# Exponentials in neighbouring pairs, eleven heads instead of eighteen with a column of ones, and a new order of steps

## The chip, the core and the metric

The kernel runs on one core of a Trainium2 chip. The metric is the device time of one execution in microseconds (us); of several runs the median counts. A core has five engines that run side by side: TensorE (PE, with its weight loads as a row of their own, PEld), VectorE (DVE), ScalarE (ACT), GpSimd (POOL) and SyncE (SP), which issues the transfers here. Each works through a fixed row of instructions and waits where data or a buffer is missing.

## The reference

The kernel computes pooled attention and then a token and channel mixer:

```python
# q, k, v: (4, 8, 1152, 64); w_tok1 (576, 256), w_tok2 (256, 576), w_ch1 (512, 1536), w_ch2 (1536, 512)
q_pool = q.reshape(B, H, S // 2, 2, D).mean(axis=3)
scores = np.matmul(q_pool, k.transpose(0, 1, 3, 2)) / np.sqrt(D)
attn = np.exp(scores - scores.max(-1, keepdims=True))
attn = attn / (attn.sum(-1, keepdims=True) + 1e-9)
x = (attn @ v).transpose(0, 2, 1, 3).reshape(B, S // 2, H * D)
h = np.maximum(x.transpose(0, 2, 1) @ w_tok1, 0) @ w_tok2
u = x + h.transpose(0, 2, 1)
out = u + np.maximum(u @ w_ch1, 0) @ w_ch2          # (4, 576, 512)
```

There are 32 heads (4 batches of 8) with 1152 keys, 576 pooled queries and 64 channels each.

## The kernel before, in words

All matrix products run in a 32-bit format that keeps fewer bits of each number than float32, so each operand is split into a high part and the rest, and a product is the sum of two or three matmuls.

**A head.** The keys stand in 9 chunks of 128, the queries in two halves of 288. One step `s` of `main` (0 to 8) takes two of the 18 pairs of half and chunk. PE computes the scores of each pair with keys on the partitions (line 756, two matmuls of 288 columns; the second also subtracts the row's maximum). ACT takes the exponential twice: once as full float32 into the tile PF (called `pf`, line 766), once rounded into `ph` (line 769). DVE or POOL forms the rest `pl = pf - ph` (line 773; the helper `both` leaves the choice of the engine to the plan). PE then multiplies `ph` and `pl` with the values `vv` (line 798) and adds up over the 9 chunks in the PSUM tile `o`.

**The sum over keys**, which divides each row, is had in two ways. Heads in the list `IN_PV` put a column of ones into `vv`: POOL saves the column that was there in `V0` and overwrites it (lines 615 and 617), and PE needs a third matmul of 288 columns for each pair, with that saved column as its one-column weight (`o<-ph,v`, 18 in a head). The others let DVE add up the 9 chunks in PF, in three thirds of 96 queries for each half (`tensor_reduce`, line 780, 6 in a head); since this leaves one number for each of the 128 partitions, PE adds these up with a column of ones (line 827, 5 matmuls in a head, each of which stands as two instructions in the trace). IN_PV has 18 heads: 0 to 3 and the odd ones from 5 to 31.

`finish` turns the result back (line 820, 5 matmuls, two instructions each), and DVE computes the denominator `den`, its reciprocal `rd` and the scaled result `u` (lines 832 to 842). The maxima of the rows are found ahead of each head by matmuls (line 691) into a ring of three PSUM tiles `r`, which DVE reduces (line 693). After each four heads comes a token mix (lines 858 to 901): ACT and DVE or POOL split `u` into `big` tiles, PE multiplies with the token weights (line 873), and again (line 891), and DVE adds to `u`. The channel mixer (lines 966 to 1030) comes after all heads.

**The order.** Nothing is issued in the order of the code. `step` records each operation with an engine, an assumed cost, a due time and the data it reads and writes. `Plan.run` then places the steps, earliest start first and due time next, and so writes each engine's row when the program is built. The table `DUE` at the head of the file shifts the due times. POOL steps and those DVE steps that are marked `shared` are planned so that they don't overlap. On the chip each engine follows its row and waits for semaphores.

Of the kernel before, what the change touches and what calls it, by code (L numbers as in the profile page):

```python
# [10 lines left out]
F32 = mybir.dt.float32  # L11
# [3 lines left out]
ALU = mybir.AluOpType  # L15
AX = mybir.AxisListType
# [6 lines left out]
PE, ACT, DVE, POOL, DMA, HOST = range(6)  # L23
# [7 lines left out]


DUE = {
    "scores": -1.4,
    "p_lo": 0.02,
    "sum": -2.82,
    "pv": 1.78,
    "o": -107.46,
    "finish": 5.54,
    "max": -22.72,  # L40
    "max_each": 0.53,
    "prep": -32.49,
    "v": 9.58,
    "stack": 29.51,
    "stack_2": 96.51,
    "mix": 9.83,
    "mix_x": 6.03,
    "w_tok": -27.04,
    "w_tok_each": 7.34,
    "sum_each": 1.2,  # L50
    "pv_lo": 0.54,
    "lo_first": 7.78,
    "max_first": -120.52,
    "max_second": 37.69,
    "scores_each": -10.71,
    "p_hi": 0.84,
    "pv_one": -0.04,
    "finish_each": -14.96,
    "den_sum": -47.39,
    "x_lo": 5.05,  # L60
    "x": -54.79,
    "den": -45.22,
    "rd": -27.39,
    "u": 18.75,
    "u_each": 75.19,
    "max_of": 7.22,
    "max_row": -32.02,
    "max_first_each": -127.47,
    "q_pool": -3.78,
    "q_turn": 1.79,  # L70
    "k_each": 1.45,
    "k_hi": -42.28,
    "k_lo": 1.7,
    "q_hi": -79.72,
    "q_lo": 70.53,
    "load_kq": -48.02,
    "load_v": -163.1,
    "v_lo": -10.5,
    "load_w_tok": 117.45,
    "mix_x_lo": 3.96,  # L80
    "mix_1": 3.17,
    "mix_t": 2.11,
    "mix_2": 2.45,
    "mix_u": -79.91,
    "w_ch": 235.24,
    "w_ch_each": -64.39,
    "ut_0": -4.75,
    "ut_1": -50.96,
    "stay": 0.78,
}  # L90


# [145 lines left out]
def kernel(  # L238
# [24 lines left out]
    P = 128  # L263
    SQ = S // 2
    NK = S // P
# [16 lines left out]
    due = DUE  # L282
    WARM = 8
    KEEP = (0, 1, 2, 3)
    UNSTACKED = 1
    IN_PV = (0, 1, 2, 3, *range(5, 32, 2))
    CUT = 3
    FOLDS = 114
    LO = (None,) * 9
# [25 lines left out]
        return 65 + 0.521 * n  # L315

    def pool_(n):
        return 150 + 2.1 * n

    def both(n, fn, *args, on=None):  # L320

# [89 lines left out]
    QD = many(early, 2, [P, P], F32R, "qd")  # L411
    MH = fix.tile([P, P], F32R, name="mh")
    OT = many(fix, 2, [P, SQ], F32, "ot")
    PF = fix.tile([P, 2 * NK, HF], F32, name="pf")
    SUM = fix.tile([P, 2, HF], F32, name="sum")
    REST = words(SUM).rearrange("p f x -> p (f x)")[:, 0:2 * J]

# [316 lines left out]
    def main(h, t0):  # L734
        i3, i2 = h % 3, h % 2
        stacked = [(KK[i3], QQ[i3]), (K2[i2][0:D + 1], Q2[i2][0:D + 1])]
        ready = [(x, i3, y) for x in ("qq", "kk") for y in range(2)] + [("k2", i2), ("q2", i2)]

        plain = [(x[0:D], y[0:D]) for x, y in (
            (KHI, QHI[0]), (KLO, QHI[0]), (KHI, QLO[0]))]  # L740
        plain.append((K2[0][D:D + 1], Q2[0][D:D + 1]))
        seen = [(x, y) for x in ("kh", "kl") for y in range(3)]
        seen += [(x, 0, y) for x in ("qh", "ql") for y in range(2)]
        for s in range(NS):
            t = t0 + s
            units = [divmod(2 * s + i, NK) for i in range(2)]
            st = Buf("s")
            for i, (fq, c) in enumerate(units):
                terms, read = stacked, ready
                if h == 0 and s < UNSTACKED:  # L750
                    terms, read = plain, seen
                read = read + [("row", i2, x) for x in ((0, 1, 2), (2, 3, 4))[fq]]

                def scores(st=st, i=i, fq=fq, c=c, terms=terms):
                    for n, (w, x) in enumerate(terms):
                        te.matmul(  # L756
                            at(st)[:, i, 0:HF], w[:, c * P:(c + 1) * P],
                            x[:, fq * HF:(fq + 1) * HF],
                            start=(n == 0), stop=(n == len(terms) - 1))

                step(PE, len(terms) * mm(HF), scores, t + due["scores"] + i * due["scores_each"],
                     read,
                     [(st, i)], [st] if i == 0 else [])
            ph, pl = Buf("ph"), Buf("pl")
            pf = PF[:, 2 * s:2 * s + 2]
            step(ACT, act_ps(2 * HF), lambda pf=pf, st=st: sc.activation(  # L766
                pf, at(st)[:, :, 0:HF], AF.Exp, scale=ESC), t,
                [(st, 0), (st, 1)], [("pf", s)])
            step(ACT, act_ps(2 * HF), lambda ph=ph, st=st: sc.activation(  # L769
                at(ph), at(st)[:, :, 0:HF], AF.Exp, scale=ESC), t + due["p_hi"],  # L770
                [(st, 0), (st, 1)], [ph], [ph])
            pv = h in IN_PV
            both(2 * HF, lambda e, pf=pf, ph=ph, pl=pl: e.tensor_sub(  # L773
                at(pl), pf, f(at(ph))), t + due["p_lo"], [("pf", s), ph], [pl], [pl],
                on=LO[s])
            if s in (4, NS - 1) and not pv:
                fq = s // 5
                for y in range(CUT):
                    cs = slice(y * HF // CUT, (y + 1) * HF // CUT)
                    step(DVE, 65 + 1.83 * NK * HF // CUT, lambda fq=fq, cs=cs: ve.tensor_reduce(  # L780
                        SUM[:, fq, cs],
                        PF[:, fq * NK:(fq + 1) * NK, cs].rearrange("p c x -> p x c"),
                        axis=AX.X, op=ALU.add), t + due["sum"] + y * due["sum_each"],
                        [("pf", x) for x in range(fq * 4, fq * 4 + 5)], [("sum", fq, y)])
            for i, (fq, c) in enumerate(units):
                if c == 0:
                    o, parts = Buf("o"), []
                terms = [(ph, VV[i2], P), (pl, VV[i2], P)]
                if pv:
                    terms.insert(1, (ph, V0[i2], 1))  # L790
                for n, (x, w, m) in enumerate(terms):
                    new, end = not parts, (c, n) == (NK - 1, len(terms) - 1)
                    key = (o, "new") if new else (o, c, n)
                    read = [x, ("v0" if m == 1 else "vv", i2)]
                    if not new:
                        read += parts if end else parts[:1]
                    step(PE, mm(HF),
                         lambda o=o, x=x, w=w, m=m, i=i, c=c, new=new, end=end: te.matmul(  # L798
                             at(o)[0:m], w[:, c], at(x)[:, i], start=new, stop=end),
                         t + due["pv"] + (x is pl) * due["pv_lo"] + (m == 1) * due["pv_one"], read, [key], [o] if new else [])  # L800
                    parts.append(key)
                if c == NK - 1:
                    step(ACT, act_ps(HF), lambda o=o, fq=fq: sc.copy(  # L803
                        OT[i2][:, fq * HF:(fq + 1) * HF], at(o)), t + due["o"],
                        parts, [("ot", i2, fq)])
# [321 lines left out]
```

## Time and profile before

| | |
|---|---|
| Three runs | 962.26, 963.37, 965.88 us (median 963.37) |
| The profiled execution | 965.31 us |
| Its span, first to last instruction | 963.5 us |
| Mean granted clock of TensorE | 0.978 of full speed |
| Busy | PE 97%, DVE 73%, ACT 53%, POOL 37% |
| 0 to 60 us | start: first head, weights of the token mix |
| 60 to 640 us | heads 1 to 31 and the token mixes |
| 640 to 963.5 us | last token mix, channel mixer |

The busy time of PE counts matmuls from start to end, and they overlap in the pipeline. So PE reads as busy even where small gaps lie between the starts. What a matmul costs is read from the distance of the starts in the timeline, not from its duration.

### The profile page before, as it was taken

The numbers are of one execution on the slowest core, as the hardware profiler recorded it, in microseconds if no ns is written. First come the engines' busy times: TensorE is split into PE (matmuls) and PEld (weight loads), VectorE is DVE, ScalarE is ACT, GpSimd is POOL, SyncE is SP. The second block draws the span as 40 slices with busy tenths as digits, with TensorE's granted clock in tenths as the row PEclk, the third lists the DMA queues.
The fourth block names the chain that finished last, engine by engine and source line by source line (L and its number), as shares of the span: only waits on it lengthen the run. The fifth ranks groups of instructions, "written<-read, shape, count | busy, mean of one in ns | idle before, by whom it ended". The sixth has DMA issues, their size and how long they took to land.

```text
span 963.5 us, 15874 instructions
## 1 busy us (share of the span) xinstructions
PE 934.6 (97%) x5852; PEld 845.2 (88%) x5852; DVE 703.5 (73%) x1268; ACT 514.3 (53%) x1038; POOL 353.4 (37%) x309
## 2 busy tenths in 40 slices
PE   9979899999999999999999999999999999999997
PEld 4767799899999999888899999998999999999996
DVE  6799999899899899989998989988882212121211
ACT  1657687687677676776766767755441111111110
POOL 0444366584584673655655646330000000000000
PEclk7789999999999999999999999999999999999999
DMA  6775656465465475365454533124430101000001
GB/s 137 202 171 121 138 113 146 97 141 126 95 151 118 93 162 118 87 136 117 100 127 95 125 69 87 45 89 133 151 110 1 66 1 33 0 34 0 32 2 33
DMA packets 89844, 91.54 MB, mean 95 GB/s; under 512 B 43884, under 2 KB 68840, under 8 KB 89768
## 3 DMA queue, kind: packets, MB, share of 16 engines
q1 hardware_dynamic: 89768, 90.54, 38.9%
q8 instruction: 46, 0.75, 0.3%
q14 instruction: 30, 0.25, 0.1%
HBM read 43.25 MB, written 4.72 MB: 50 GB/s over the span
## 4 chain that ended last, share of the span: by engine, by line
PE 77%; DVE 17%; ACT 3%; DMA 2%; issue 1%; DVEq 0%; SPq 0%; ACTq 0%
PE r L988 16%; PE o L798 14%; PE s L1016 12%; PE s L756 10%; PE r L691 7%; DVE mx L693 6%; DVE pl L773 3%; PE r L820 3%; PE r L891 3%; DVE sum L780 3%; PE o L1016 3%; PE r L873 2%; PE r L827 2%; DMA kk<-kl 1%; PE r L559 1%
## 5 line engine op out<-in xcount | busy, mean ns | idle before, releaser
L773 POOL TENSOR_TENSOR pl<-pf,ph 128x576 fp32r<-128x576 f32 x187 | 267.7, 1452 | 155.2 <-ACT ph L769 107.7
L766 ACT ACTIVATE pf<-s 128x576 f32<-128x576 f32 x288 | 189.4, 659 | 87.6 <-PE s L756 80.3
L693 DVE TENSOR_REDUCE mx<-r 128x1 f32<-128x384 f32 x384 | 198.6, 553 | 17.3 <-PE r L691 14.5
L769 ACT ACTIVATE ph<-s 128x576 fp32r<-128x576 f32 x288 | 187.9, 659 | 0.0
L756 PE MATMUL s<-qq,kk 128*128 128x288 f32 x574 | 169.8, 308 | 1.8 <-ACT ph L769 1.6
L756 PE MATMUL s<-q,k 65*128 65x288 f32 (+1 forms) x576 | 167.4, 302 | 0.0
L996 DVE SCALAR_TENSOR_TENSOR h<-r,h 128x384 fp32r<-128x384 f32 x72 | 40.1, 557 | 166.9 <-ACT h L994 166.8
L780 DVE TENSOR_REDUCE sum<-pf 128x96 f32<-128x864 f32 x84 | 147.4, 1763 | 0.9 <-ACT pf L766 0.8
L798 PE MATMUL o<-ph,vv 128*128 128x288 f32 x576 | 145.5, 307 | 0.9 <-ACT ot L803 0.9
L691 PE MATMUL r<-kk,qq 128*128 128x384 f32 x372 | 131.7, 369 | 14.1 <-DVE mx L693 6.8
L994 ACT ACTIVATE h<-r 128x384 fp32r<-128x384 f32 x72 | 35.4, 492 | 197.0 <-PE r L988 196.8
L798 PE MATMUL o<-pl,vv 128*128 128x288 f32 x576 | 139.4, 299 | 0.3 <-DVE pl L773 0.3
L1016 PE MATMUL s<-w,h 128*128 128x512 f32 x504 | 130.8, 394 | 0.0
L756 PEld LDWEIGHTS s<-qq,kk 128*128 128x128 f32 x574 | 110.8, 193 | 6.0 <-ACT ph L769 4.0
L756 PEld LDWEIGHTS s<-q,k 65*128 65x128 f32 (+1 forms) x576 | 111.5, 194 | 0.6 <-issue 0.6
L798 PEld LDWEIGHTS o<-ph,vv 128*128 128x128 f32 x576 | 101.2, 192 | 11.1 <-ACT ot L803 2.6
L988 PE MATMUL r<-big,w 128*128 128x384 f32 x576 | 109.0, 337 | 0.0
L1016 PEld LDWEIGHTS s<-w,h 128*128 128x128 f32 x504 | 93.4, 188 | 16.5
L988 PEld LDWEIGHTS r<-big,w 128*128 128x128 f32 x576 | 101.7, 188 | 3.8 <-DVE h L996 0.2
L798 PEld LDWEIGHTS o<-pl,vv 128*128 128x128 f32 x576 | 100.0, 191 | 1.6 <-DVE pl L773 0.6
L773 DVE TENSOR_TENSOR pl<-pf,ph 128x576 fp32r<-128x576 f32 x101 | 93.4, 930 | 2.1 <-ACT ph L769 1.5
L691 PEld LDWEIGHTS r<-kk,qq 128*128 128x128 f32 x372 | 71.4, 195 | 26.3 <-DVE mx L693 10.7
(129 smaller groups left out, 1274.7 us busy)
## 6 DMA issues: line engine op xcount, KB each, us to landing
raw<-in_moe_w_ch_dram SPq DMA_DIRECT2D x24, 512.0 KB, 3.8
kk<-kh SPq DMA_DIRECT2D x32, 288.0 KB, 3.4
kk<-kl SPq DMA_DIRECT2D x32, 288.0 KB, 4.9
qq<-qh SPq DMA_DIRECT2D x64, 144.0 KB
vn<-in_v_dram SPq DMA_DIRECT2D x32, 288.0 KB, 2.8
k<-kk SPq DMA_DIRECT2D x31, 288.0 KB, 5.1
kn<-in_k_dram SPq DMA_DIRECT2D x30, 288.0 KB
qn<-in_q_dram SPq DMA_DIRECT2D x32, 256.0 KB, 7.6
```

The source lines that it names most:

```text
L691: step(PE, mm(SP3), lambda ps=ps, w=w, x=x: te.matmul(at(ps)[:, 0:SP3], w, x, start=True, stop=True), t, read, [ps], [ps])
L693: step(DVE, dve(SP3), lambda ps=ps, m=m: ve.tensor_reduce(m, at(ps)[:, 0:SP3], axis=AX.X, op=ALU.max), t + due["max_of"], [ps], [key])
L756: te.matmul(at(st)[:, i, 0:HF], w[:, c * P:(c + 1) * P], x[:, fq * HF:(fq + 1) * HF], start=(n == 0), stop=(n == len(terms) - 1))
L766: step(ACT, act_ps(2 * HF), lambda pf=pf, st=st: sc.activation(pf, at(st)[:, :, 0:HF], AF.Exp, scale=ESC), t, [(st, 0), (st, 1)], [("pf", s)])
L769: step(ACT, act_ps(2 * HF), lambda ph=ph, st=st: sc.activation(at(ph), at(st)[:, :, 0:HF], AF.Exp, scale=ESC), t + due["p_hi"], [(st, 0), ...
L773: both(2 * HF, lambda e, pf=pf, ph=ph, pl=pl: e.tensor_sub(at(pl), pf, f(at(ph))), t + due["p_lo"], [("pf", s), ph], [pl], [pl], on=LO[s])
L780: step(DVE, 65 + 1.83 * NK * HF // CUT, lambda fq=fq, cs=cs: ve.tensor_reduce(SUM[:, fq, cs], PF[:, fq * NK:(fq + 1) * NK, cs].rearrange(" ...
L798: lambda o=o, x=x, w=w, m=m, i=i, c=c, new=new, end=end: te.matmul(at(o)[0:m], w[:, c], at(x)[:, i], start=new, stop=end),
L988: te.matmul(at(ps)[:, 0:GT], w[:, c], x[:, c], start=(c == 0 and n == 0), stop=(c == NC4 - 1 and n == 2))
L994: step(ACT, act_ps(GT), lambda: sc.activation(at(h)[:, 0], at(ps)[:, 0:GT], AF.Relu), t, [ps], [h])
L996: step(DVE, dve(GT), lambda: ve.scalar_tensor_tensor(out=at(h)[:, 1], in0=at(ps)[:, 0:GT], scalar=0.0, in1=f(at(h))[:, 0], op0=ALU.max, op ...
L1016: te.matmul(at(ps), a[:, x * P:(x + 1) * P], w, start=(fi == 0 and m == 0), stop=(fi == NF - 1 and m == 2))
```

## The change

It has four parts.

1. PF gets a last dimension of two: the exponentials of the same query of two neighbouring chunks lie side by side. ACT writes each of its two chunks with a distance of 8 bytes from element to element, and `pl` reads PF with the same distance. The middle step (`s == 4`), whose two chunks belong to different halves, gets two places of its own, each with a second element that is set to zero once at the start (a new memset of 576 elements).
2. DVE's sum runs over the five pairs of a half, so over 10 elements for each query in place of 9, with the two of a pair next to each other.
3. IN_PV keeps heads 0 to 3 and every fourth from 5 to 29: 11 heads, not 18. Seven heads go from the column of ones to the sum on DVE, among them head 31, the last.
4. The table of due times has other numbers, and the planner's assumed cost of POOL's elementwise operations is 2.3 ns an element, not 2.1.

```diff
 DUE = {
-    "sum": -2.82,
+    "sum": -2.85,
...
-    "p_hi": 0.84,
+    "p_hi": -1.72,
...
-    IN_PV = (0, 1, 2, 3, *range(5, 32, 2))
+    IN_PV = (0, 1, 2, 3, *range(5, 32, 4))
...
     def pool_(n):
-        return 150 + 2.1 * n
+        return 150 + 2.3 * n
...
-    PF = fix.tile([P, 2 * NK, HF], F32, name="pf")
+
+
+    PF = fix.tile([P, 2 * 5, HF, 2], F32, name="pf")
+    ve.memset(PF[:, 4:6, :, 1], 0.0)
...
-            pf = PF[:, 2 * s:2 * s + 2]
+            if s == 4:
+                pf = PF[:, 4:6, :, 0]
+            else:
+                pf = PF[:, s + (s > 4)].rearrange("p x t -> p t x")
...
-                    step(DVE, 65 + 1.83 * NK * HF // CUT, lambda fq=fq, cs=cs: ve.tensor_reduce(
+                    step(DVE, 65 + 1.15 * 10 * HF // CUT, lambda fq=fq, cs=cs: ve.tensor_reduce(
                         SUM[:, fq, cs],
-                        PF[:, fq * NK:(fq + 1) * NK, cs].rearrange("p c x -> p x c"),
-                        axis=AX.X, op=ALU.add), t + due["sum"] + y * due["sum_each"],
+                        PF[:, 5 * fq:5 * fq + 5, cs].rearrange("p s x t -> p x s t"),
+                        axis=AX.XY, op=ALU.add), t + due["sum"] + y * due["sum_each"],
```

In the whole program the built rows hold these numbers of instructions, before and now: matmuls with the saved column 324 and 198; sums on DVE 84 and 126; matmuls of a column of ones with the sums 70 and 105 (two instructions each); `pl` on DVE 101 and 87, on POOL 187 and 201; rests of the values (`vv<-vn,vv`) on DVE 12 and 4, on POOL 20 and 28; rests of `u` (`big<-u,big`) on DVE 10 and 15, on POOL 30 and 25; saved columns and memsets of ones on POOL 18 and 11 each.

The line numbers of the new kernel are 3 higher than before from PF on to the exponentials and 6 higher after them (line 773 is 779, 820 is 826, 873 is 879, 988 is 994).

The first place is PE's row before the change where head 31, the last one, ends: `fold` and `ot` are its result's turn, `big` the operands of the last token mix's first product, `t1h` and `t1l` those of the second product of the mix before it, `ut` and `w` the channel mixer's.

```order
L891 MATMUL r_80<-t1l,w2h 128x256
L820 MATMUL r_81<-fold_110,ot_106 128x65 x5
L891 MATMUL r_82<-t1h,w2h 128x256
L891 MATMUL r_82<-t1h,w2l 128x256
L891 MATMUL r_82<-t1l,w2h 128x256
L891 MATMUL r_80<-t1h,w2h 128x256
```

PE's row now, in the same place.

```order
L897 MATMUL r_81<-t1l,w2h 128x256
L826 MATMUL r_82<-fold_110,ot_106 128x64
L833 MATMUL r_82<-ones,sum 128x1 x5
L826 MATMUL r_82<-fold_110,ot_106 128x64 x4
L879 MATMUL r_81<-big_72,big_70 128x256
L879 MATMUL r_81<-big_72,big_71 128x256
L879 MATMUL r_81<-big_73,big_70 128x256
```

Before, 21 matmuls of line 891 and 12 of the channel mixer (line 988) stood between the turn of the last head and the first product that needs that head's result. Now that product follows at once; the matmuls of line 891 stand ahead of the turn, those of the channel mixer behind the product.

The second place is DVE's row there before the change: from the denominator of head 31 to the first rests of its `u`.

```order
L901 TENSOR_TENSOR u_66<-r_80,u_66 128x256
L832 TENSOR_SCALAR den_131<-r_81 128x5
L834 RECIPROCAL rd_133<-den_131 128x5
L901 TENSOR_TENSOR u_66<-r_82,u_66 128x256
L839 TENSOR_TENSOR u_66<-r_81,rd_133 128x4x64
```

DVE's row now, from that denominator on.

```order
L838 TENSOR_SCALAR den_132<-r_82 128x5
L361 SCALAR_TENSOR_TENSOR v_6350<-raw_6348,v_6350 128x512
L840 RECIPROCAL rd_134<-den_132 128x5
L358 SCALAR_TENSOR_TENSOR v_6351<-raw_6349,v_6351 128x512
L845 TENSOR_TENSOR u_66<-r_82,rd_134 128x4x64
L361 SCALAR_TENSOR_TENSOR v_6351<-raw_6349,v_6351 128x512
L867 TENSOR_TENSOR big_73<-u_66,big_72 128x256 x4
```

Three operations on the channel mixer's weights (lines 358 and 361, 512 elements each) now stand between the steps from `den` to the first rest, for which PE's next matmul waits.

The third place is DVE's row before the change at about 50 us, where the token mix's weights (`w`) are converted between the second head's steps.

```order
L773 TENSOR_TENSOR pl_159<-pf,ph_157 128x576
L352 TENSOR_SCALAR w_152<-w_152 128x256
L352 TENSOR_SCALAR w_153<-w_153 128x256
L355 TENSOR_SCALAR w_152<-w_152 128x256
L355 TENSOR_SCALAR w_153<-w_153 128x256
L358 SCALAR_TENSOR_TENSOR w_152<-u_66,w_152 128x256
```

DVE's row now, at the second pair of these weights.

```order
L696 TENSOR_REDUCE mx_127<-r_81 128x1
L661 TENSOR_REDUCE mh<-rm 128x1
L352 TENSOR_SCALAR w_153<-w_153 128x256
L696 TENSOR_REDUCE mx_127<-r_80 128x1
L696 TENSOR_REDUCE mx_127<-r_82 128x1
L696 TENSOR_REDUCE mx_127<-r_81 128x1
L355 TENSOR_SCALAR w_153<-w_153 128x256
```

The conversions of two weights no longer stand as a pair: they come one by one between the maxima, and later in the row.

## Rows read from the trace of the kernel before

**Rows 1.** The page: busy time of each engine; shares of the chain that ended last.

```profile
PE 934.6 (97%) x5852; PEld 845.2 (88%) x5852; DVE 703.5 (73%) x1268; ACT 514.3 (53%) x1038; POOL 353.4 (37%) x309
PE 77%; DVE 17%; ACT 3%; DMA 2%; issue 1%; DVEq 0%; SPq 0%; ACTq 0%
```

**Rows 2.** Stretches: window, length, busy PE PEld DVE ACT POOL, PEclk, DMA.

```profile
60.00:640.00 580.00, 565.07 (x3996) 521.29 (x3997) 538.25 (x950) 417.12 (x842) 328.96 (x279) 0.99 0.49 112
```

**Rows 3.** PE's timeline, end of a head with DVE's sums: start, us, what.

```profile
184.03 0.43 PE L798 MATMUL o<-ph,v 128*1 128x288 f32 x2
184.29 0.33 PE L820 MATMUL r<-fold,ot 128*128 128x64 f32 x2
184.46 1.23 PE L827 MATMUL r<-ones,sum 128*128 128x1 f32 x10
185.55 1.08 PE L820 MATMUL r<-fold,ot 128*128 128x64 f32 x8
...
186.71 0.48 PE L580 MATMUL r<-ident,qp 128*128 128x128 f32 x2
```

**Rows 4.** Groups by line, whole span: operation, count | busy us, mean ns | idle before.

```profile
L693 DVE TENSOR_REDUCE mx<-r 128x1 f32<-128x384 f32 x384 | 198.6, 553 | 17.3 <-PE r L691 14.5
L780 DVE TENSOR_REDUCE sum<-pf 128x96 f32<-128x864 f32 x84 | 147.4, 1763 | 0.9 <-ACT pf L766 0.8
L654 DVE TENSOR_REDUCE mh<-mx 128x4 fp32r<-128x12 f32 x31 | 4.9, 158 | 0.3
```

**Rows 5.** Groups by line, whole span: what reads or writes elements 8 bytes apart, and like operations.

```profile
L358 DVE SCALAR_TENSOR_TENSOR v<-raw,v 128x512 uint32<-128x512 uint32 x24 | 16.5, 689 | 0.4
L951 DVE TENSOR_TENSOR w<-v,w 128x512 fp32r<-128x512 f32 x20 | 13.8, 690 | 5.3 <-ACT w L950 5.2
L351 ACT ACTIVATE v<-raw 128x512 f32<-128x512 f32 x24 | 16.1, 670 | 15.8 <-DMA raw<-in_moe_w_ch_dram 14.6 <-POOL w L951 0.7 <-issue 0.3
L950 ACT CAST w<-v 128x512 fp32r<-128x512 f32 x24 | 14.8, 618 | 20.0 <-DVE v L361 19.9
```

**Rows 6.** Groups by line, whole span: elementwise work that changes its engine, and a memset.

```profile
L773 POOL TENSOR_TENSOR pl<-pf,ph 128x576 fp32r<-128x576 f32 x187 | 267.7, 1452 | 155.2 <-ACT ph L769 107.7 <-PE o L798 12.6 <-DVE w L951 10.9
L773 DVE TENSOR_TENSOR pl<-pf,ph 128x576 fp32r<-128x576 f32 x101 | 93.4, 930 | 2.1 <-ACT ph L769 1.5
L613 DVE TENSOR_TENSOR vv<-vn,vv 128x576 fp32r<-128x576 f32 x12 | 10.0, 835 | 0.1
L861 DVE TENSOR_TENSOR big<-u,big 128x256 fp32r<-128x256 f32 (+1 forms) x10 | 7.1, 723 | 0.0
L435 DVE MEMSET vv<- 128x512 f32 x1 | 0.5, 485 | 0.1
```

**Rows 7.** PE's waits, 80 to 640 us: us in total, times, longest.

```profile
PE r L691 <- DVE mx L693: 5.8, 9, 2.1
```

**Rows 8.** Timeline of all engines at 51.8 us, then the clock of the stretch behind.

```profile
51.80 6.12 DVE L352 TENSOR_SCALAR w<-w 128x256 f32<-128x256 f32 x2 [0.62 <-ACT w L351]
53.62 4.14 POOL L773 TENSOR_TENSOR pl<-pf,ph 128x576 fp32r<-128x576 f32 x3
60.71 0.44 PE L691 MATMUL r<-kk,qq 128*128 128x384 f32 x1 [3.38 <-DVE u L842]
60.70:68.10 7.40, 6.36 (x25) 5.49 (x26) 6.74 (x13) 4.37 (x9) 1.67 (x1) 0.54 0.72 141
```

**Rows 9.** Timeline of DVE where the last head ends: start, us, what.

```profile
638.91 0.17 DVE L832 TENSOR_SCALAR den<-r 128x5 f32<-128x5 f32 x1 [0.44 <-PE r L820]
639.11 0.19 DVE L834 RECIPROCAL rd<-den 128x5 f32<-128x5 f32 x1
639.67 0.41 DVE L839 TENSOR_TENSOR u<-r,rd 128x256 f32<-128x256 f32 x1
```

**Rows 10.** Stretch behind the end of a head of rows 3; columns as in rows 2.

```profile
187.40:190.80 3.40, 3.40 (x16) 3.38 (x16) 2.69 (x9) 2.26 (x7) 0.39 (x1) 0.50 0.47 121
```

More of the change, by code (lines that the diff above doesn't have):

```diff
@@ L33 @@
 DUE = {
-    "scores": -1.4,
+    "scores": -1.44,
     "p_lo": 0.02,
-    "sum": -2.82,
[L37 to L40, printed above, removed]
-    "max_each": 0.53,
[L42 to L49, printed above, removed]
-    "sum_each": 1.2,
[L51 to L55, printed above, removed]
@@ L56 @@
-    "p_hi": 0.84,
[L57 to L65, printed above, removed]
-    "max_of": 7.22,
[L67 to L79, printed above, removed]
@@ L80 @@
-    "mix_x_lo": 3.96,
-    "mix_1": 3.17,
-    "mix_t": 2.11,
[L83 to L89, printed above, removed]
+    "sum": -2.85,
+    "pv": 1.83,
+    "o": -106.67,
+    "finish": 6.19,
+    "max": -23.88,
+    "max_each": 0.53,
+    "prep": -20.71,
+    "v": 9.57,
+    "stack": -37.51,
+    "stack_2": 124.61,
+    "mix": 9.71,
+    "mix_x": 4.12,
+    "w_tok": -4.59,
+    "w_tok_each": 7.51,
+    "sum_each": 1.2,
@@ new lines @@
+    "pv_lo": 0.65,
+    "lo_first": 27.69,
+    "max_first": -99.69,
+    "max_second": -11.98,
+    "scores_each": -10.2,
+    "p_hi": -1.72,
+    "pv_one": -0.14,
+    "finish_each": -28.2,
+    "den_sum": -76.93,
+    "x_lo": 35.19,
+    "x": -35.05,
+    "den": -14.07,
+    "rd": -28.27,
+    "u": -6.85,
+    "u_each": 50.98,
+    "max_of": 7.22,
+    "max_row": -22.16,
+    "max_first_each": -144.64,
+    "q_pool": -2.06,
+    "q_turn": 1.75,
+    "k_each": 0.76,
+    "k_hi": -36.13,
+    "k_lo": -37.61,
@@ L90 @@
+    "q_hi": -119.82,
+    "q_lo": 95.45,
+    "load_kq": -13.24,
+    "load_v": -96.57,
+    "v_lo": -10.03,
+    "load_w_tok": 243.74,
+    "mix_x_lo": 2.72,
+    "mix_1": 3.26,
+    "mix_t": 2.11,
+    "mix_2": 2.48,
+    "mix_u": -64.01,
+    "w_ch": 237.69,
+    "w_ch_each": -54.79,
+    "ut_0": -5.5,
+    "ut_1": 0.95,
+    "stay": 4.87,
 }
```

## The prediction

> **What bounds the kernel now.** I read the page's busy times and chain first. PE is busy for 97% of the span and holds 77% of the chain, DVE holds 17% [rows 1]. Then I cut the span into stretches. Between 60 and 640 us PE is busy for 565 of 580 us and DVE for 538 (93%), ACT for 417, POOL for 329 [rows 2]. So in the attention two engines are nearly full, PE a little more than DVE. The timeline of PE shows its matmuls one behind the other: two of 288 columns start 0.26 us before the next kind (184.03 to 184.29), so one costs 0.13 us there, whatever its recorded 0.43 us for the pair [rows 3]. The waits come last: what PE waits for in the attention is mostly DVE, and there the reduction of the maxima, which has to free a ring tile (5.8 us in 9 waits) [rows 7].
>
> From this follows the rule for the sum below: a matmul taken off PE is worth its distance to the next one, and work taken off DVE is worth only the part of PE's waits that it shortens.
>
> The sum is made against the profiled execution (965.3 us, span 963.5 us, 1.8 us around it). That execution lies 1.9 us above the median of the runs, so I carry the difference over to the median, 963.4 us. A difference under 0.5%, 4.8 us, I call no change: that is about what a measurement of this kernel can tell.
>
> **The change part by part.**
>
> *Matmuls with the saved column.* Seven heads lose 18 each, 126 in all, at 0.13 us [rows 3]: -16.4 us. All of them lie on PE, in stretches in which PE hardly waits.
>
> *Matmuls of ones with the sums.* Seven heads gain ten instructions each (five matmuls, each in two). In the timeline ten of them take from 184.46 to 185.55, 1.09 us [rows 3]: +7.6 us. The turn of the result (line 820) changes from 65 to 64 columns, which I count as nothing.
>
> *The sums on DVE.* Before there are 84 at 1763 ns for 864 elements, each 1152 bytes from the one before [rows 4]. No row shows a reduction over pairs. The bounds: reductions whose elements lie side by side take 158 ns for 12 elements and 553 ns for 384, so 1.06 ns for each further one; the old sums come to (1763 - 158) / 852 = 1.88 ns. For 960 elements that gives 158 + 948 x 1.06 = 1163 ns at best and 1943 ns at worst. I take 1163, since half of the steps now go to the neighbour, and since the row of 384 elements is the one whose data lie as in a pair. Then 126 sums need 146.5 us against 148.1: 1.6 us less on DVE, though there are half as many again. The lower bound is the same number: nothing in the rows reduces faster.
>
> [...]
>
> *Elements 8 bytes apart.* DVE reads such elements already: 689 ns for 512 (line 358) against 690 ns for like work on neighbours (line 951) [rows 5]. So `pl` on DVE costs nothing more. ACT reads them in 670 against 618 ns [rows 5], 0.1 ns an element; no row shows ACT writing so, or POOL reading so. For ACT's write I take nothing; the bounds are 0 and the ratio of the sums, 1.88 / 1.06 = 1.77, and the nearest row, 670 / 618 = 1.08, lies by the lower one. What hides an 8% longer write (15 us on 288 of them) is ACT's idle time, 163 of 580 us [rows 2]. For POOL I take nothing too; it idles for 251 us.
>
> *Work that moves from DVE to POOL.* 14 `pl` less at 930 ns, 8 rests of the values less at 835, 5 rests of `u` more at 723 [rows 6]: -13.0 - 6.7 + 3.6 = -16.1 us, with the sums -17.7 us on DVE. POOL gets about 14 x 1.45 = 20 us more for `pl` and less than that for the rest, on 329. Both have no direct price. But DVE's idle time in the attention grows from 42 to 59 us, and heads become more alike. A head on DVE's sums asks 6 x 1.76 = 10.6 us more of DVE than one with ones; now 7.0. Before, such a head needed more DVE time than PE gives it and the next made up for it; now the surplus is smaller, though three follow each other. I let a third of PE's 5.8 us of waits go: -1.9 us; bounds -5.8 and, as the order is new throughout, +5.
>
> *The start.* [...] The new row has the conversions one by one and in another place. [...]
>
> *The memset of PF.* It stands ahead of the memset that the first matmuls wait for. 576 elements at the rate of line 435 (485 ns for 512) [rows 6]: +0.5 us, and the chain begins there.
>
> *The handover.* Before, PE had 33 matmuls between the last head's turn and the first product that needs it. Now there is none, and DVE has to do den 0.17, a weight operation 0.69, rd 0.19, another 0.69, u 0.41, a third 0.69 and the first rest 0.72 [rows 5, 6, 9]: 3.6 us in which PE idles. The matmuls that covered it are still there, earlier or later, so this is all loss. A gap of this size was followed by the lower level of the clock [rows 8]; I add 1.7 us, what 3.4 us at half speed cost [rows 10]. +5.3 us; bounds +2 (DVE's steps overlap with earlier PE work) and +7.
>
> Sum: -16.4 + 7.6 - 1.9 - 3.4 + 0.5 + 5.3 = -8.3 us. The profiled execution would come to 957.0 us, the median to 955.1: **955 us**. The orders of SP's transfers change too; in the attention PE's waits for them are far under the ones above, and I count nothing.
>
> **The rivals.**
>
> *A: the new order eats part of it.* Neither waits nor collisions shrink, only the matmuls count: -8.3 + 5.3 = -3.0, 960 us. For it: PE and DVE are both over 90%, and any order leaves waits. Against it: DVE gets 17.7 us lighter.
>
> *B, slower: pairs don't help DVE.* At 1943 ns the sums need 244.8 us, 96.7 more; less the 16.1 that went to POOL that is +80.6 on DVE, which has 41.7 us idle: it becomes the bound and adds 39 us. 1002 us. It decides from about 1.63 us a sum, where (148.1 + 16.1 + 41.7) / 126 fills DVE. It is also the case in which the change doesn't do what it says. For it: the step from pair to pair is still long. Against it: 1.06 ns for neighbours.
>
> *C: ACT's write at distance costs 1.77 times.* 659 ns becomes 1166 in 288 exponentials, 146 us: ACT at 563 of 580 us. I price it by three times PE's present waits for DVE, which is 93% full: +17, 972 us. Against it: 8% in the nearest row.
>
> *D: the sums of ones let the clock fall.* Behind the block of rows 3, with narrow matmuls for 3 us, the clock fell to its lower level for 3.4 us [rows 10]; it happened so twice (again at 525.3 us) in 14 such blocks, 1.7 us each. There are 21 now. In the same share that is one more, within the range; in all, 19 more and +32 us, 987. Five more use up the gain.
>
> *E: POOL and DVE collide more.* POOL has 22 more two-input operations beside DVE. Two more events like that of rows 8 than before: 955.1 + 3.4 + 13.6 = 972 us. [...]
>
> **How the numbers follow.** The forecast has 0.71, with a range of its own of 947 to 961; A 0.15, B 0.04, C 0.03, D 0.03, E 0.04. The range that should hold 8 in 10 is 945 to 965: it takes in A and the bounds of the waits, the start and the handover, and leaves out B to E. Faster by over 0.5% (under 958.6 us): 0.64 of the forecast and 0.06 of A, 0.70. No change: 0.07, 0.09 of A and 0.02 of E, 0.18. Slower (over 968.2): B, C, D and half of E, 0.12.
>
> **What would show it.** In the profile after: 198 matmuls with the saved column and 210 instructions of ones; the sum's mean near 1.16 us (B: 1.9); the exponential into PF still near 660 ns (C: over 1.0); DVE busy some 18 us less before the handover; one gap on PE of 3 to 4 us behind the last turn, with `big` as what ended it; PE's waits for the maxima under 5 us. Stretches at half clock behind the narrow blocks, more than three, would show D; conversions or `pl` on DVE of over 3 us would show E. I am wrong if the sum or the write is dear, or if PE's waits grow by more than the 8.8 us that the matmuls give.

## The result and the profile after

The changed kernel takes 969.4 us (median of 20 runs, 963.3 to 977.0) against 964.1 for the kernel before in the same rounds (20 runs): ratio 1.0065, 95% interval 1.0041 to 1.009. It is slower by 0.65%; the forecast was 955, faster by 0.9%.

The page of the changed kernel, busy times and chain, against [rows 1]:

```profile
PE 930.7 (96%) x5796; PEld 850.0 (88%) x5796; DVE 679.5 (70%) x1289; ACT 522.3 (54%) x1038; POOL 384.9 (40%) x317
PE 73%; DVE 10%; DMA 7%; ACT 7%; issue 2%; SPq 0%; ACTq 0%; DVEq 0%
```

PE has 56 rows fewer (126 taken off, 70 added), DVE is 24.0 us lighter, and the span is longer all the same (971.4 us). On the chain DVE went from 17% to 10% and DMA from 2% to 7%. The groups that answer to [rows 4 to 6], columns as there:

```profile
L786 DVE TENSOR_REDUCE sum<-pf 128x96 f32<-128x960 f32 x126 | 143.2, 1140 | 1.3 <-ACT pf L772 0.6
L772 ACT ACTIVATE pf<-s 128x576 f32<-128x576 f32 x288 | 200.3, 704 | 2.5 <-DVE sum L786 1.5 <-PE s L759 0.7
L779 POOL TENSOR_TENSOR pl<-pf,ph 128x576 fp32r<-128x576 f32 x201 | 293.7, 1479 | 196.1 <-ACT pf L772 112.3 <-PE o L804 31.5 <-DMA q<-mt 16.1
L779 DVE TENSOR_TENSOR pl<-pf,ph 128x576 fp32r<-128x576 f32 x87 | 79.9, 921 | 3.5 <-ACT pf L772 2.5 <-PE s L759 0.6
```

A sum takes 1140 ns for 960 elements, the write in pairs 704 ns (659 before), and 14 `pl` went to POOL. The new thing stands in PE's waits, 80 to 640 us, as in [rows 7]:

```profile
PE r L694 <- DMA qq<-qh: 13.2, 8, 3.1
PE r L694 <- DVE mx L696: 3.3, 6, 0.7
```

The wait for the maxima fell from 5.8 to 3.3 us; in its place PE waits 13.2 us for copies of queries, which are not among its waits of 0.2 us and more before (there it waits 2.0 us for copies, all of keys). One of these places, SP's queue of the changed kernel (start, us, line, what), then PE, then the stretch behind (columns as in [rows 2]):

```profile
351.71 0.69 SPq L632 DMA_DIRECT2D kk<-kh  x1
352.45 0.59 SPq L632 DMA_DIRECT2D kk<-kl  x1
353.14 0.88 SPq L632 DMA_DIRECT2D kk<-kh  x1
354.07 1.76 SPq L632 DMA_DIRECT2D kk<-kl  x1
355.93 3.47 SPq L632 DMA_DIRECT2D qq<-qh  x4
...
359.20 0.29 PE L759 MATMUL s<-q,k 65*128 65x288 f32 x1
361.39 0.41 PE L694 MATMUL r<-kk,qq 128*128 128x384 f32 x1 [1.90 <-DMA qq<-qh]
...
361.39:365.30 3.91, 3.91 (x17) 3.91 (x18) 2.90 (x5) 2.86 (x5) 3.63 (x4) 0.58 1.26 252
```

Two heads' keys (288 KB a copy) stand ahead of all the queries. The second pair of `kk` copies is the next head's and not urgent; the queries behind it are, and PE idles 1.9 us and then runs most of 3.9 us at half clock (0.58 of full speed in the mean). SP's row has this order before heads 15, 19, 23, 27 and 31, and nowhere in the kernel before. Around four of these five places the clock falls to half (0.50 to 0.51 of full speed for 3.4 us from 286.9, 362.0 and 437.1 us on, 0.50 for 6.8 us from 512.2 on). The other four places, and below them a sixth wait for queries, at a place without this order:

```profile
285.55 0.41 PE L694 MATMUL r<-kk,qq 128*128 128x384 f32 x1 [1.64 <-DMA qq<-qh]
436.92 0.47 PE L694 MATMUL r<-kk,qq 128*128 128x384 f32 x1 [1.74 <-DMA qq<-qh]
513.42 0.66 PE L694 MATMUL r<-kk,qq 128*128 128x384 f32 x1 [3.08 <-DMA qq<-qh]
588.51 0.59 PE L694 MATMUL r<-kk,qq 128*128 128x384 f32 x2 [1.93 <-DMA qq<-qh]
...
208.86 0.76 PE L694 MATMUL r<-kk,qq 128*128 128x384 f32 x3 [2.03 <-DMA qq<-qh]
```

The five places wait 10.3 us together. The waits of 1.93 and 2.03 us have no half clock behind them, so half clock does not follow every gap of this size. The kernel has one more stretch at half clock in the attention, 3.4 us (0.50) from 239.2 us on, next to a wait of 1.25 us for DVE's `sum`.

The handover, which answers to [rows 9]: PE's timeline, then the stretch at half clock.

```profile
641.43 1.08 PE L826 MATMUL r<-fold,ot 128*128 128x64 f32 x8
644.81 0.51 PE L879 MATMUL r<-big,big 128*128 128x256 f32 x2 [2.29 <-ACT big L864]
646.25 4.00 PE L879 MATMUL r<-big,big 128*128 128x256 f32 x17 [0.94 <-DVE big L867]
...
645.30:652.10 6.80, 5.86 (x26) 5.85 (x26) 5.36 (x13) 2.76 (x6) 0.02 (x1) 0.50 0.37 119
```

### The profile page after: what moved, and what is told of

Same layout as the page of the kernel before. It is cut to its first block, busy times and chain, and to the rows that moved or that the text cites. A ratio compares the mean times of both kernels' runs of the same rounds, so it can differ in the third digit from the quotient of the medians.

```text
span 971.4 us, 15995 instructions
## 1 busy us (share of the span) xinstructions
PE 930.7 (96%) x5796; PEld 850.0 (88%) x5796; DVE 679.5 (70%) x1289; ACT 522.3 (54%) x1038; POOL 384.9 (40%) x317
## 4 chain that ended last, share of the span: by engine, by line
PE 73%; DVE 10%; DMA 7%; ACT 7%; issue 2%; SPq 0%; ACTq 0%; DVEq 0%
PE o L804 14%; PE r L994 13%; PE s L759 13%; PE s L1022 10%; PE r L694 8%; DMA qq<-qh 4%; PE r L826 3%; DMA raw<-in_moe_w_ch_dram 3%; PE r L879 3%; PE r L833 2%; PE o L1022 2%; ACT pf L772 2%; DVE mx L696 2%; ACT ph L775 2%; DVE sum L786 1%
## 5 line engine op out<-in xcount | busy, mean ns | idle before, releaser
L779 POOL TENSOR_TENSOR pl<-pf,ph 128x576 fp32r<-128x576 f32 x201 | 293.7, 1479 | 196.1 <-ACT pf L772 112.3
L696 DVE TENSOR_REDUCE mx<-r 128x1 f32<-128x384 f32 x384 | 195.0, 548 | 47.6 <-PE r L694 44.8
L772 ACT ACTIVATE pf<-s 128x576 f32<-128x576 f32 x288 | 200.3, 704 | 2.5 <-DVE sum L786 1.5
L759 PE MATMUL s<-qq,kk 128*128 128x288 f32 x574 | 172.9, 313 | 2.9 <-ACT pf L772 2.5
L759 PE MATMUL s<-q,k 65*128 65x288 f32 (+1 forms) x576 | 169.8, 306 | 0.0
L694 PE MATMUL r<-kk,qq 128*128 128x384 f32 x372 | 125.0, 365 | 20.3 <-DMA qq<-qh 13.5
L786 DVE TENSOR_REDUCE sum<-pf 128x96 f32<-128x960 f32 x126 | 143.2, 1140 | 1.3 <-ACT pf L772 0.6
L804 PE MATMUL o<-ph,vv 128*128 128x288 f32 x576 | 141.5, 305 | 1.5 <-ACT ot L809 1.4
L759 PEld LDWEIGHTS s<-q,k 65*128 65x128 f32 (+1 forms) x576 | 113.8, 198 | 0.6 <-issue 0.6
L1022 PEld LDWEIGHTS s<-w,h 128*128 128x128 f32 x504 | 93.1, 188 | 16.2
L779 DVE TENSOR_TENSOR pl<-pf,ph 128x576 fp32r<-128x576 f32 x87 | 79.9, 921 | 3.5 <-ACT pf L772 2.5
```

What stands on the lines that cost most here:

```text
L694: step(PE, mm(SP3), lambda ps=ps, w=w, x=x: te.matmul(at(ps)[:, 0:SP3], w, x, start=True, stop=True), t, read, [ps], [ps])
L696: step(DVE, dve(SP3), lambda ps=ps, m=m: ve.tensor_reduce(m, at(ps)[:, 0:SP3], axis=AX.X, op=ALU.max), t + due["max_of"], [ps], [key])
L759: te.matmul(at(st)[:, i, 0:HF], w[:, c * P:(c + 1) * P], x[:, fq * HF:(fq + 1) * HF], start=(n == 0), stop=(n == len(terms) - 1))
L779: both(2 * HF, lambda e, pf=pf, ph=ph, pl=pl: e.tensor_sub(at(pl), pf, f(at(ph))), t + due["p_lo"], [("pf", s), ph], [pl], [pl], on=LO[s])
L786: step(DVE, 65 + 1.15 * 10 * HF // CUT, lambda fq=fq, cs=cs: ve.tensor_reduce(SUM[:, fq, cs], PF[:, 5 * fq:5 * fq + 5, cs].rearrange("p s ...
L1022: te.matmul(at(ps), a[:, x * P:(x + 1) * P], w, start=(fi == 0 and m == 0), stop=(fi == NF - 1 and m == 2))
```

## The experiments

Three theories: T1, SP's order of copies costs the time; T2, the moved work and added sums cost it in any order; T3, ACT's longer write holds the buffers of the scores. All ratios are to the kernel before in the same rounds, with 95% intervals. Line numbers of the variants are shifted by some lines.

### The order of the copies

Queries first: SP's row alone, all other rows as in the changed kernel.

```diff
+    order = plan.run()
+    for h in range(1, NH):
+        place = {s: n for n, s in enumerate(order)}
+        last = max(place[s] for s in copies[h - 1, "qq"])
+        late = sorted((s for s in copies[h, "kk"] if place[s] < last), key=place.get)
+        if late:
...
+            order[last + 1:last + 1] = late
+            for s in late:
+                order.remove(s)
```

> The changed kernel with SP's row alone changed: copies of a head's keys that stood ahead of the last copy of the head before it's queries are moved right behind that copy; the rows of PE, DVE, ACT and POOL are word for word those of the changed kernel. T1: PE's waits for qq under 3 us (13.5 in the changed kernel), the five spells at half clock behind them gone (about 2 us each): 952 to 958 us. T2 and T3: under 5 us of difference to the changed kernel, 965 to 970 us.

954.9 us, ratio 0.9896 (0.9872 to 0.992): 14.5 us below the changed kernel's median and faster than before. SP's queue and PE at the place shown above, then PE's first waits (80 to 620 us), of this run:

```profile
348.20 2.11 SPq L635 DMA_DIRECT2D qq<-qh  x2
350.40 0.65 SPq L635 DMA_DIRECT2D kk<-kh  x1
351.10 0.66 SPq L635 DMA_DIRECT2D kk<-kl  x1
351.81 2.44 SPq L635 DMA_DIRECT2D qq<-qh  x2
...
353.64 0.30 PE L762 MATMUL s<-q,k 65*128 65x288 f32 x1
353.77 0.34 PE L697 MATMUL r<-kk,qq 128*128 128x384 f32 x1
...
PE r L697 <- DMA qq<-qh: 2.7, 3, 1.0
```

The same matmul now follows its neighbour at once, and the clock holds: from 71.2 us to the handover no stretch is at half clock (1.00 in the mean of 60 to 620 us). T1 is shown; T2 and T3, which gave this run under 5 us, fall.

The two profiled executions (973.2 and 953.2 us) have the same instructions of PE in the same order, so one can be taken from the other matmul by matmul. Around the five places the changed kernel falls behind by 3.2, 3.4, 3.3, 5.6 and 1.9 us, 17.4 of 19.9 us in all. Of the rest, 2.8 us stand ahead of the first place, where the rows of SP are the same too, and differ from run to run; 1.1 us stand at the handover; 1.5 us are made up between the places.

Three of the five places repaired, as a dose:

```diff
-    for h in range(1, NH):
+    for h in (23, 27, 31):
```

> As the kernel with the queries first, but for the last three (heads 23, 27 and 31) of the five heads alone; before heads 15 and 19 the keys still go ahead of the queries, as in the changed kernel. T1 with a price for each such place of 14.5 / 5 = 2.9 us: 954.9 + 2 x 2.9 = 960.7 us, with two waits for qq of 1.5 to 3 us and half clock behind them at about 285 and 361 us of the span, none behind the other three places. If only the longest wait (3.1 us, head 27's) mattered: 955 us.

959.3 us, ratio 0.9946 (0.9915 to 0.9977): 4.4 us over the full repair, 5.8 expected; the two intervals just touch. The two places left wait as before. Half clock follows the second (a mean of 0.94 over 340 to 370 us), not the first; another 3.4 us of it, from 311.2 us on (0.96 over 280 to 320), stand at a wait of 1.71 us for a copy from `q`:

```profile
280.80 0.41 PE L697 MATMUL r<-kk,qq 128*128 128x384 f32 x1 [2.11 <-DMA qq<-qh]
358.10 0.41 PE L697 MATMUL r<-kk,qq 128*128 128x384 f32 x1 [1.89 <-DMA qq<-qh]
```

### The table and the work belong together

The changed kernel with the whole table of before; the kernel before with the new table; the changed kernel with one number of the old one; the repaired kernel with 18 heads:

```diff
-    "prep": -20.71,
+    "prep": -32.49,
...
-    IN_PV = (0, 1, 2, 3, *range(5, 32, 4))
+    IN_PV = (0, 1, 2, 3, *range(5, 32, 2))
```

> The changed kernel, with the table of due times of the kernel before (the pairs, the 11 heads with a column of ones and the planner's price for POOL stay as changed). SP's copies of queries then stand ahead of the keys of the same head again. T1 (the new due times order SP's copies so that keys of the next head go ahead of this head's queries, and PE waits for the queries and then runs at half clock): PE's waits for qq go from 13.5 us in 9 to under 3, about 955 us, ratio 0.99. T2 (the added sums, the later POOL work and the two s buffers cost it, whatever the order): about 965 us. T3 (the conversion written in pairs takes 704 ns and holds the s buffers): about 965 us, with the waits for pf as they were (2.5 us at s, 9.7 at the weight loads).

> The kernel before with the new table of due times alone: no pairs, 18 heads with a column of ones, the planner's price for POOL as before. T1: slower than before by what the order costs, 10 to 18 us, so 972 to 982 us, with PE waiting 10 us or more for qq and half clock behind it. T2 and T3: the order alone is worth under 4 us either way, 960 to 968 us.

> The changed kernel with one number of its table set back: prep from -20.71 to -32.49, so keys and queries of a pair of heads are turned 11.8 us earlier in the planner's time. No head's keys then go ahead of the queries of the head before (5 heads in the changed kernel); the other rows shift a little too. T1 (SP's order of copies costs the time): PE's waits for qq under 4 us and no half clock behind them, 954 to 962 us. T2 and T3 (the added sums, or ACT's longer conversions, cost it): 964 to 972 us.

> The kernel with the queries first (954.9 us), with 18 heads holding a column of ones again in place of 11: PE gets 126 x 0.130 = 16.4 us of columns back and gives up 70 x 0.109 = 7.6 us of matmuls of ones, DVE loses 42 sums of 1.14 us. T1: 954.9 + 8.8 = about 964 us (960 to 970, since the planner shifts rows). T2 (the 42 added sums cost as much as they save): 952 to 957 us.

In this order:

- the changed kernel with the old table: 997.4 us, 1.0361 (1.0318 to 1.0405);
- the kernel before with the new table: 980.3 us, 1.0159 (1.0121 to 1.0197);
- the changed kernel with the old `prep`: 987.5 us, 1.0266 (1.0223 to 1.0309);
- the repaired kernel with 18 heads: 975.9 us, 1.016 (1.0112 to 1.0208).

All four take longer than the kernel before, and in none do a head's keys stand ahead of the queries of the head before it. My expectations failed for the first, third and fourth, and the second's time came out without its reason (3.0 us of waits for `qq`, not 10). What the profiles show is that the planner answers a changed number by moving other work: in the first, third and fourth 124, 120 and 135 of the `pl` are on DVE (87 in the changed kernel), and PE's waits spread over many places. So undoing the table was no test of T1, since it undoes everything else the table sets; moving SP's rows alone was. How much of each run's loss comes from which row stays open.

### The pairs alone

```diff
-    PF = fix.tile([P, 2 * NK, HF], F32, name="pf")
+    PF = fix.tile([P, 2 * 5, HF, 2], F32, name="pf")
```

> The kernel before with the neighbouring pairs alone: 18 heads with a column of ones, the table and the planner's prices as before, so every engine's row is that of the kernel before, but for the memset and the form of pf. DVE gets 84 x 0.6 = 50 us lighter, ACT 288 x 0.045 = 13 us heavier, PE's work is the same. T1: PE was not held by DVE's sums, so 960 to 966 us, the same as before within 0.5%. T3 (the slower conversion holds the s buffers): PE's waits for pf and ph grow by over 5 us, 968 to 976 us. If DVE did hold PE: 950 to 958 us.

964.7 us, ratio 1.0014 (0.9987 to 1.0041): no change, with DVE at 663.7 us (703.5 before) and ACT at 521.2 (514.3). T3's sign did not come: PE's waits for `pf` and `ph` are 1.8 us against 1.6 before, not 5 more. The run has the longer write and 40 us less on DVE at once, so a small cost of the one could hide behind a small gain of the other.

### What a matmul is worth

Without the saved column (11 heads, repaired kernel; the same for seven heads of the kernel before; the latter with the pairs):

```diff
-    end=end: te.matmul(
+    end=end: m == 1 or te.matmul(                            # 198 left out
+    end=end: m == 1 and h in range(7, 32, 4) or te.matmul(   # 126 left out
```

> The kernel with the queries first (954.9 us), with the 198 matmuls left out that add the column saved from v in the 11 heads with a column of ones (that part of the output is then missing); all other rows are word for word the same. It measures the first term of the sum by itself. If a matmul of PE's row is worth its start-to-start distance there: 198 x 0.130 = 25.7 us less, 929 us. If waits take part of it back, as after the change: 935 to 945 us.

> The kernel before, with the 126 matmuls of the saved column left out in the seven heads that lose their column of ones in the change (heads 7, 11, ... 31; that part of the output is then missing); nothing else is changed. It measures the prediction's first term at its own place. If PE sets the pace: -16.4 us, 948 us. If DVE or the chain of conversions takes it back as it did with the queries first: -2 to -5 us, 959 to 962 us.

> The kernel before with the pairs (964.7 us alone) and, in the seven heads that lose their column of ones in the change, without the 126 matmuls of the saved column (964.1 us alone; that part of the output is missing): the old order, with PE 16.4 us and DVE 50 us lighter. If the two are bounds in turn and pay together: 952 to 958 us. If neither the sums nor these matmuls are on the path in the old order: 961 to 965 us.

In this order:

- the repaired kernel without the 198 matmuls: 952.3 us, 0.9856 (0.9821 to 0.9891), 2.6 us of 25.7;
- the kernel before without 126: 964.1 us, 1.0006 (0.9987 to 1.0025), nothing of 16.4 (its profiled execution is the shortest of its 12);
- the kernel before without 126 and with the pairs: 963.6 us, 0.9985 (0.9965 to 1.0005), nothing that can be told.

The differences between variants here and below are those of medians from different rounds; by the ratios they differ from that by up to 1.5 us (3.9 us for the 2.6), and each is known to 3 to 4 us. The clock is a part of it. What the mean granted clock of a run lacks to full speed, times the run's time, is an estimate of the time lost to half clock. As a mean of the runs it is 25.7 us without the 126 matmuls and 20.9 in the kernel before in the same rounds, but 11.9 without the 198 and 17.5 in the repaired kernel. So by this estimate the clock took back some 5 us of the first saving, and may account for all of the second.

That so little is left I had not expected. Head 23, from the copy of the head before's result to its own, in the kernel before and without the column; head 25 in the repaired kernel and without it (columns as in [rows 2]):

```profile
472.64:492.95 20.31, 19.53 (x139) 17.29 (x138) 18.12 (x36) 13.73 (x30) 8.57 (x7) 1.00 0.38 93
...
468.26:488.52 20.26, 18.32 (x121) 15.94 (x120) 18.07 (x36) 13.67 (x30) 8.51 (x7) 1.00 0.37 92
...
500.73:521.45 20.72, 20.68 (x152) 18.98 (x150) 19.17 (x43) 14.43 (x32) 11.64 (x10) 1.00 0.59 131
...
495.45:515.66 20.21, 20.05 (x134) 17.96 (x133) 19.00 (x43) 14.45 (x31) 11.65 (x10) 1.00 0.58 135
```

18 rows are gone from each, 2.3 us at 0.13, and the head is 0.05 and 0.51 us shorter. In the repaired kernel's head DVE is busy for 19.0 of 20.2 us, nearly full; in that of the kernel before for 18.1 of 20.3. I then made DVE lighter, by shorter sums and by maxima over half of the columns, each with and without the column, and issued the column twice:

```diff
-                        PF[:, 5 * fq:5 * fq + 5, cs].rearrange(
+                        PF[:, 5 * fq:5 * fq + 2, cs].rearrange(
...
-            m, at(ps)[:, 0:SP3], axis=AX.X, op=ALU.max)
+            m, at(ps)[:, 0:SP3 // 2], axis=AX.X, op=ALU.max)
...
-    end=end: te.matmul(at(o)[0:m], ...)
+    end=end: [te.matmul(at(o)[0:m], ...) for _ in range(1 + (m == 1))]
```

> The kernel with the queries first (954.9 us), with DVE's sums over 2 of 5 steps alone (83 us less on DVE, the sums are not the reference's); PE's work is the same. If DVE holds it: 940 us or less. If PE is the bound there: 951 to 956 us, the same.

> The kernel with the queries first, without the 198 matmuls of the saved column (952.3 us), and with each of DVE's 126 sums over 2 of its 5 steps only (384 elements in place of 960, so the sums are not the reference's): some 0.66 us less each, 83 us less on DVE, all rows in their places. If DVE takes over as PE gets lighter: PE's waits shrink and the saved matmuls show, 928 to 938 us. If the loop of scores, conversions and products, or SP's copies, hold PE: 948 to 953 us.

> The kernel with the queries first (954.9 us), with DVE's maxima over half of their columns alone, and PE's work as it is. If PE's work is the bound as soon as DVE is not: 945 to 952 us, since the waits for mx (2.5 + 2.6 us) and those spread over the heads go. If nothing waits for DVE: 953 to 956 us.

> The kernel with the queries first, without the 198 matmuls of the saved column (952.3 us), with DVE's 432 maxima over the first half of their columns alone (192 of 384, so the row shifts before the exponential are not the reference's): some 0.2 us less each, 86 us less on DVE, 2.4 us in a head. If DVE's maxima hold PE in the heads with a column: the missing matmuls show, 928 to 940 us. If the chain of conversions or the copies do: 947 to 953 us.

> The kernel with the queries first (954.9 us), with each of the 198 matmuls of the saved column issued twice (that part of the output counts twice); PE's row gets 198 x 0.130 = 25.7 us longer. If PE sets the pace: 980 us. If something else sets it by as much as leaving them out showed: under 965 us.

- Short sums: 954.7 us, 0.9912 (0.9879 to 0.9946), and without the column 948.5, 0.9855 (0.9825 to 0.9885). By the ratios that is nothing, and in head 25 only one of these sums lies.
- Half maxima: 948.6 us, 0.9839 (0.9812 to 0.9866), and without the column 944.4, 0.9791 (0.9757 to 0.9825). Lighter maxima are worth 6 to 8 us, but the column then shows only 4.2 of its 25.7.
- The column twice: 968.4 us, 1.0047 (1.0025 to 1.007), 13.4 of 25.7.

Head 25 again, with half maxima without the column, and with the column twice:

```profile
496.87:516.62 19.75, 19.09 (x133) 17.63 (x131) 16.20 (x43) 14.40 (x31) 11.68 (x10) 1.00 0.62 139
...
517.89:540.43 22.54, 22.54 (x168) 20.27 (x167) 19.22 (x43) 14.45 (x31) 10.74 (x9) 1.00 0.54 120
```

With DVE at 16.2 us and the column gone the head is still 19.75 us long. No engine but PE is near full there, and PE's waits of over 0.15 us come to 0.7 us, for the maxima (0.5) and for ACT's `pf` (0.2); in the whole run those for `pf` grow to 6.8 us in 13 waits, from 2.8 in 5 with the queries first. The rest lies in small gaps: in the rows above, 134 in 20.21 us without the column are 0.151 us each, 152 in 20.72 us with it 0.136. So work that is added to PE's row costs 1.8 of 2.3 us in this head and about half of its length in the whole kernel, and work that is removed hardly anything. What sets the small gaps, and which row would have to move first, stays open.

### The matmuls of ones

```diff
-    te.matmul(turned()[:, c, D:D + 1], sums[:, qc(c)], ones, start=True, stop=True)
+    [te.matmul(...) for _ in range(2)]
```

> The kernel with the queries first (954.9 us), with each of the 105 matmuls of ones issued twice with the same result; they stand as 210 rows in the trace, 109 ns each; all other rows are the same. It measures the second term of the sum by itself. If they cost their start-to-start distance: 210 x 0.109 = 22.9 us more, 978 us. If the narrow blocks pull the clock down: over 985 us. If they lie in PE's idle time: under 970 us.

999.0 us, 1.0339 (1.0301 to 1.0376): 44 us over the repaired kernel, of which the rows are 22.9. The clock makes up the rest: by the estimate above it takes 42.6 us of these runs and 17.5 of the repaired kernel's. These 25 us and the 22.9 are together a little more than the 44, so the estimate is good to some 4 us. One end of a head, and the stretch behind it:

```profile
182.58 2.34 PE L836 MATMUL r<-ones,sum 128*128 128x1 f32 x20
184.79 1.08 PE L829 MATMUL r<-fold,ot 128*128 128x64 f32 x8
...
186.20:189.60 3.40, 3.40 (x16) 3.40 (x15) 3.40 (x7) 1.98 (x4) 1.55 (x2) 0.50 0.00 0
```

Here PE is busy all along before the clock falls. Behind 15 of the 21 blocks (the last at the handover) a stretch at half clock begins within 2.1 us of the last matmul of ones. With single blocks none of 21 is followed so in the changed kernel or the repaired one, but for the handover, and 2 of 14 in the kernel before.

### The handover

Two rows of DVE behind the rests of `big`; and, better, the last head's reciprocal, product, casts and rests right behind its sum `den` (the diff):

```diff
+    block = [*rest, *ahead[0::2], *ahead[1::2]]   # rd, u, 4 casts, 4 rests
...
+    for s in block:
+        order.remove(s)
+    order[n0 + 1:n0 + 1] = block                  # n0: place of den
```

> As the run before, and in DVE's row at the handover the two last head steps (subtraction of the low part and its rest) stand behind the four rests that the mix waits for. T1: PE's wait for big at the handover falls from 2.29 + 0.94 us to about 2, with the half clock behind it as it is: 1 to 2 us below the run before, 950 to 957 us. If nothing in DVE's row sets it (ACT's big is last): the same as the run before within 0.5 us. T2 and T3: 963 to 970 us.

> The kernel with the queries first (954.9 us), and at the handover the last head's reciprocal and product, the four casts of big on ACT and the four rests of big on DVE stand right behind the sum den, ahead of two conversions of weights (0.68 + 0.65 us) on DVE and a cast of weights (0.62 us) on ACT. PE's waits for big, 2.29 + 0.65 us, fall to about 1.3 in all, and the half clock behind them may go: 951 to 954 us. If the transposition itself or the clock sets the handover: 954 to 957 us.

958.9 us, 0.9931 (0.99 to 0.9962), and 955.8, 0.992 (0.9891 to 0.9949): no gain that can be told. In the first the moved rows read their weights after the next transfer had taken their place (DVE waits 1.94 us for `raw`), so that part of the output is not the reference's. In the second the waits for `big` fell as meant, from 2.29 and 0.65 us to 1.4, and another stands behind it:

```profile
PE r L977 <- DVE h L1007: 2.2, 1, 2.2
PE r L884 <- ACT big L867: 1.4, 1, 1.4
```

DVE, which now does its weight conversions later, is late with `h`; that one causes the other was not tried. The fastest kernel that computes the reference stays the changed one with the queries first.

## Why the prediction was wrong

The step that failed is the last sentence of the sum: "The orders of SP's transfers change too; in the attention PE's waits for them are far under the ones above, and I count nothing." I read a small wait in the trace before as a property of the transfers. It was one of their order, and the change replaces the order. Nor was it far under the others: 2.0 us in two waits for copies of keys, where I let 1.9 us of waits for the maxima go. The term was +14.5 us, the difference of the two medians (16 by the ratios). It was there to be read: the new order of SP's row shows the next head's keys ahead of a head's queries five times, and for none of them did I ask who waits for what stands behind.

Point by point:

- The sum over pairs: 1163 ns forecast, 1140 measured; 1.04 ns for each further element against 1.88 before. Rival B is out. With every second step to the neighbour the sum runs at the rate of the maxima, 1.06 ns, whose elements all lie side by side.
- The write at distance: nothing forecast, 45 ns each measured, 13 us on ACT (8.0 us of its busy time; operations overlap a little: 288 of 704 ns are 202.8 us and stand as 200.3), and the pairs alone left the time where it was. Rival C is out.
- DVE: 17.7 us less forecast, 24.0 measured. Most of the difference lies in the rests of `u`: I took 5 more at 723 ns, +3.6 us; measured are 15 in 5.8 us against 10 in 7.1, 1.3 us less. PE's waits for the maxima fell by 2.5 us where I said 1.9. Right in kind.
- The memset: PE's first wait for `vv` went from 1.5 to 2.1 us, +0.6 for +0.5. Right.
- The start: the sum's -3.4 us is half of 6.8, an estimate from [rows 8] (3.4 us of gap on PE, 3.4 lost at half clock), taken at even odds; no run shows this term. A slow conversion beside POOL's work was still there (3.85 us for 256 elements at 62.21 us, where POOL has three `pl` in 4.22 us; 6.12 us for two before; the median of the nine on `w` is 0.31). That POOL's work slows it was not tried. PE's gap at 60.7 us is 2.2 us, 3.4 before, and it ends on another engine, a copy. The stretches at half clock behind it add up to 6.8 us in both. So of the 3.4 us that I took off the gap shows 1.2 and the clock nothing.
- The handover: 3.2 us idle (3.6 forecast) and 6.8 us at half clock, 3.4 lost (1.7 forecast). Right in kind, 1.3 us short.
- Rival D: no stretch at half clock stands behind the narrow blocks of the attention. It did not come, but the run with the ones twice shows it at twice the block. (The narrow matmuls of [rows 3] last 2.3 us, not the 3 that I wrote.)
- Rival E: `pl` 921 ns on DVE and 1479 on POOL, 930 and 1452 before. It did not come. One conversion of over 3 us, my sign for it, is there (the 3.85 us above), but the kernel before has such a place too.
- "PE's waits grow by more than the 8.8 us": this is the condition I named under which I would be wrong, and it is what happened, for a reason that I had not listed: in the profiled executions PE's gaps grow from 23.8 to 35.5 us, by 11.7.

With the failed term undone the time is 954.9 us where I forecast 955. That does not prove the sum. The rule under it, "a matmul taken off PE is worth its distance to the next one", fails by itself: 126 matmuls off PE in the kernel before gave 0.0 us and not 16.4. Nor did it pay together with 40 us less on DVE (963.6 us), so two engines that bound the kernel in turn, 97% and 93% busy as they are, do not explain it by themselves; I had both numbers and priced PE's work as if it stood alone. What came of it came with the new order: from head 24's end to head 28's the kernel before takes 74.9 us (some 1.7 of it, an estimate, for a stretch of 3.4 us at half clock) and the repaired one 72.4. That the sum met the repaired time is, as far as these runs show, luck: it is the work of the new order as a whole, and how that divides over the terms was not settled.

## What to carry to other kernels

Where a change sets a new order, read every queue's new row against the old one, transfers above all: ask for each copy that moved ahead who waits for the one behind it, and do not take a small wait of the old order for the new one's. Where two engines are over 90% busy, do not price work taken off one of them at its length: here it brought 0 to 4 us of 16 to 26, also where the other was lighter. Work added to the fuller one cost half of its length (13.4 of 25.7 us). Leave the rows out, or issue them twice, and measure. To test an order, move the rows of one queue and hold the others; a number in a planner's table moves them all.

## What the chip showed that I had not expected

- Ten narrow matmuls in a block (1.1 us) left the clock up, but for 2 of 14 in the kernel before; twenty (2.2 us) were followed by 3.4 or 6.8 us at half clock in 15 of 21 places, though PE was busy where I looked. They cost 44 us where their rows are 22.9.
- Idle gaps of 1.6 to 3.1 us on PE came with 3.4 to 6.8 us at half clock at four of the five places with late queries; two gaps of 1.93 and 2.03 us in the same trace did not. So the five late copies cost 17.4 us in the profiled executions where the waits show 10.3.
- ACT writes 576 elements 8 bytes apart in 704 ns, against 659 side by side.
